# Down products of two signs as seven block products, in a Fourier mixing and gated expert kernel

## The chip, the cores and the metric

One core of a Trainium2 chip runs the whole program. The metric is the device time of one execution in microseconds. Before the change three runs took 1185.56, 1186.44 and 1188.01 us, the median is 1186.44. The core has TensorE (PE, with its weight loads shown as PEld), VectorE (DVE), ScalarE (ACT), GpSimd (POOL) and SyncE (SP, which here only issues transfers). TensorE writes to PSUM, a memory of eight banks of 512 fp32 columns in 128 partitions; ACT and DVE read and write both PSUM and SBUF; GpSimd works in SBUF.

## The reference

The input `x` is 8 x 3136 x 256. It is mixed by a Fourier transform over the sequence and one over the features, of which the real part is kept. The 25088 rows that result go through a feed-forward block with a softmax gate and a layer norm:

```python
X = np.fft.fft(np.fft.fft(x, axis=1), axis=2).real       # (8, 3136, 256)
h = X.reshape(25088, 256) @ w_in                          # 1024 wide
e = np.exp(h - h.max(-1)); sm = e / (e.sum(-1) + 1e-9)
solu = h * sm
ln = (solu - solu.mean(-1)) / np.sqrt(solu.var(-1) + 1e-6) * g_ln
out = ln @ w_out                                          # (25088, 256)
```

## The kernel before

**Transforms.** The eight sequences are worked on as four pairs. A sequence position is n = 64 n1 + n2 with 49 values of n1 and 64 of n2. The first transform (`transform1`, L171) goes over n1 for all n2, in sixteen pieces per pair; ACT copies each (L174) and SP writes it to a scratch in DRAM, from which `turn` (L187) loads it back with n2 on the partitions, five values of k1 at a time, into tiles of the pool `gpool`. The second transform (`transform2`, L199) goes over n2 for one k1 and gives 128 tokens; ACT copies the result to `q` (L205) and a small transfer, `spread`, puts one row of it to where VectorE wants it. The transform over features is folded into `w_in` at the start, with the even and odd halves of the features kept apart.

**Units and signs.** A unit is a pair and a k1 from 0 to 24: 100 units. The sum and the difference of the even and odd halves belong to k1 and to its mirror 49 - k1. These are the two signs of a unit; each sign has 128 tokens. Units with k1 = 0 have one sign.

**A unit's way.** `up` (L227) gives the even half in two PSUM banks, then the odd half in two others; `even` (L233, DVE) adds a rank-one term and puts the even half into SBUF; `join` (L241, DVE) makes h for each sign with its row maximum; `expo` (ACT) negates the maximum (L249) and takes the exponential (L251) with its sum; `product` (L259, DVE) multiplies h into it, giving u and the sum of u; GpSimd turns that sum to minus the mean (`nmean`, L264); `square` (L271, ACT) sums the squared deviations; `stats` (five small instructions on GpSimd) makes the scale rs of each token. Then u has to be transposed: DVE transposes blocks of 32 x 32 into `v` (`turn_blocks`, L299) and 16 transfers per batch of two units move the blocks to their places in `uT` (`move_blocks`, L325, SP). `uT` holds the two signs interleaved, element by element. `down` (L331) multiplies u of one sign, 128 x 1024, by `Wo`, 1024 x 256, in eight calls that sum in a PSUM tile; ACT scales the result by rs (`scale`, L336), and `store` writes it out, sign 0 from SP, sign 1 by an indirect transfer from GpSimd (L343). The layer norm's mean is taken out of `Wo` at the start (`centre`).

**Order.** The order of the instructions on every engine is the one in which the source issues them. Each engine works off its own list strictly in that order, and semaphores are set between engines where one uses what another made or still holds. The main loop has one step per unit, and a step works on units of different ages: step i issues `store` of unit i-5, then `up` and `even` of unit i, the second transform of unit i+2, then the joins and exponentials of unit i, the first transform of the next pair (`ahead_pe`), the down products of unit i-4 (`lag = 4`), the products, squares and block transposes of unit i, the scalings of unit i-4, the moves if the batch is full, `stats` of unit i, and for the next pair its loads, mirrored additions (`add_mirror`, L131, GpSimd) and folds (`fold`, DVE) in `ahead`. The first four units (`whole = 4`) are transposed on TensorE instead (`turn_whole`, L311), as there is no time yet for the moves. PSUM is full: four banks for `up`, four for everything else (`ps_m`).

Of the kernel before, what the change touches and what calls it, by code (L numbers as in the profile page):

```python
# [35 lines left out]
def kernel(  # L36
# [34 lines left out]
    gpool = ctx.enter_context(tc.tile_pool(name="gpool", bufs=6))  # L71
# [5 lines left out]
    ps_m = ctx.enter_context(tc.tile_pool(name="ps_m", bufs=4, space=PSUM))  # L77
# [5 lines left out]
    Wo = const.tile([P, KF, D], FP32, name="Wo")  # L83
    ones = const.tile([P, P], FP32, name="ones")
# [7 lines left out]

    class Pair:
        def __init__(self, p):
            self.p = p
            self.raw, self.y, self.y0 = {}, {}, None
            self.g, self.zs = {}, {}
# [45 lines left out]
    def transform1(pr, s):  # L145
# [6 lines left out]
        if l == 0:  # L152
# [3 lines left out]
            elif c < 4:  # L156
                z = fpool.tile([P, FF], FP32, tag="u", name="z_u", bufs=2)
                pr.z = z[0:ZR].rearrange("p (l d) -> p l d", l=CH)
            else:
                pr.z = gpool.tile([P, KG, D], FP32, tag="g", name="z_g")[0:ZR, 0:CH, :]  # L160
            pr.zs[c] = pr.z
        y = pr.y[c]
        ps = ps_m.tile([P, 2, D], FP32, tag="m", name="ps1")
        if s == NH // 2 - 1:
            parts = [(ps[0:ZR, 0], y[:, l], 0), (ps[0:ZR, 1], pr.y0[:, 0], 1), (ps[0:ZR, 1], y[:, l + 1], 2)]
        else:
            parts = [(ps[0:ZR], y[:, l : l + 2], 0)]
        first = True
# [67 lines left out]
    def join(t, ps):  # L236

        t.nmax = small.tile([P, 2], FP32, tag="nmax", name="nmax")
        for s in t.signs:
            t.h[s] = fpool.tile([P, FF], FP32, tag="h", name="h", bufs=2)  # L240
            nc.vector.tensor_tensor_reduce(out=t.h[s], in0=t.ev, in1=ps, scale=1.0, scalar=-3.0e38,  # L241
                                           op0=ALU.subtract if s else ALU.add, op1=ALU.max,
                                           accum_out=t.nmax[:, s : s + 1])
# [10 lines left out]
    def product(t, s, alone):  # L254

        if s == 0:
            t.usum = small.tile([P, 2], FP32, tag="usum", name="usum")
            t.nmean = small.tile([P, 2], FP32, tag="nmean", name="nmean")
        nc.vector.scalar_tensor_tensor(out=t.u[s], in0=t.h[s], scalar=1.0, in1=t.u[s], op0=ALU.mult,  # L259
                                       op1=ALU.mult, accum_out=t.usum[:, s : s + 1])  # L260
        if alone:
            nc.scalar.mul(out=t.nmean[:, s : s + 1], in_=t.usum[:, s : s + 1], mul=-1.0 / FF)
        else:
            nc.gpsimd.tensor_scalar(out=t.nmean[:, s : s + 1], in0=t.usum[:, s : s + 1], scalar1=-1.0 / FF,  # L264
                                    scalar2=None, op0=ALU.mult)

    def square(t, s):
# [3 lines left out]
        nc.scalar.activation(out=t.h[s], in_=t.u[s], func=ACT.Square, bias=t.nmean[:, s : s + 1],  # L271
                             accum_out=t.ssq[:, s : s + 1])

    def stats(t):
# [8 lines left out]
        nc.gpsimd.tensor_scalar(out=v[:, n], in0=t.ssq[:, n], scalar1=1.0 / FF, scalar2=None, op0=ALU.mult)  # L283
# [17 lines left out]
    def turn_whole(t):  # L301
# [4 lines left out]
        for s in t.signs:  # L306
            for half in range(2):
                ps = ps_m.tile([P, n, P], FP32, tag="m", name="ps_t")
# [17 lines left out]

    def down(t, s):
        uT = t.batch.uT[:, t.w].rearrange("p c i (n s) -> p c (i n) s", s=2)
        ps = ps_m.tile([P, D], FP32, tag="m", name="ps_o")
# [28 lines left out]
    mantissa = const.tile([P, NW], I32, name="mantissa")  # L358
# [13 lines left out]
    def exponent(w, raw):  # L372
# [3 lines left out]
        unit = qpool.tile([P, NW], I32, tag="unit", name="unit", bufs=3)  # L376
# [139 lines left out]
    def ahead_pe(pr, step):  # L516
# [5 lines left out]
        if 0 <= step - 20 < NK // KG:  # L522
            turn(pr, step - 20)

    with tc.manual_schedule():
# [82 lines left out]
        def begin(i):  # L608

            cur = units[i]  # L610
            if i % 2 == 0:
                batches.append(Batch(i >= whole))
            cur.batch, cur.w = batches[-1], i % 2
            even(cur, up(cur, 0))
            cur.odd = up(cur, 1)
            if i + 2 < len(units):
                nxt = units[i + 2]
                take2(nxt, transform2(pairs[nxt.p], nxt.k1))
                spread(nxt)
# [3 lines left out]
        for i in range(len(units) + lag):  # L623
            cur = units[i] if i < len(units) else None
            old = units[i - lag] if i >= lag else None
            ahd = pairs[cur.p + 1] if cur and cur.p + 1 < NP else None
# [131 lines left out]
```

## Time and profile before

| | |
|---|---|
| median of three runs | 1186.44 us |
| the profiled execution | 1185.83 us |
| its span, first to last instruction | 1183.7 us |
| TensorE clock granted | 1.00 |
| busy: PE, DVE, ACT, POOL | 1151.6, 904.6, 679.3, 494.1 us |
| down products on PE (L331) | 693.4 us, 3136 instructions |
| up products on PE (L227) | 360.5 us, 800 instructions |

A line of the groups reads: line, engine, operation, output <- inputs, shapes, count | busy us, mean ns of one | idle time of the engine ahead of them and what ended it. One fp32 matmul call of the source is two matmul instructions, each with a weight load. The mean of one matmul includes its way through the array, which overlaps the next matmul, so the rate is read from the length of a run and not from the mean. A line of a timeline reads: start, length, engine, line, operation, output <- inputs, shapes, count [idle before it <- what ended the idle time].

### The profile page before, as it was taken

The numbers are of one execution on the slowest core, as the hardware profiler recorded it, in microseconds if no ns is written. First come the engines' busy times: TensorE is split into PE (matmuls) and PEld (weight loads), VectorE is DVE, ScalarE is ACT, GpSimd is POOL, SyncE is SP. The second block draws the span as 40 slices with busy tenths as digits, with TensorE's granted clock in tenths as the row PEclk, the third lists the DMA queues.
The fourth block names the chain that finished last, engine by engine and source line by source line (L and its number), as shares of the span: only waits on it lengthen the run. The fifth ranks groups of instructions, "written<-read, shape, count | busy, mean of one in ns | idle before, by whom it ended". The sixth has DMA issues, their size and how long they took to land.

```text
span 1183.7 us, 15921 instructions
## 1 busy us (share of the span) xinstructions
PE 1151.6 (97%) x4720; PEld 873.9 (74%) x4720; DVE 904.6 (76%) x1234; ACT 679.3 (57%) x1411; POOL 494.1 (42%) x955
## 2 busy tenths in 40 slices
PE   2999999999999999999999999999999999999998
PEld 1557777777777777778777777777777777777787
DVE  7899777777868877877768878777777887777770
ACT  4577565555646665656546656565564665655561
POOL 3035545424435435333544444442543334333433
PEclk9999999999999999999999999999999999999999
DMA  9673868746875765654774775764684453534534
GB/s 241 200 180 75 209 157 194 199 126 155 193 184 139 192 177 140 177 149 130 179 189 133 194 177 144 171 173 113 163 196 123 119 144 103 148 107 124 142 90 118
DMA packets 458454, 185.39 MB, mean 157 GB/s; under 512 B 425750, under 2 KB 440350, under 8 KB 458368
## 3 DMA queue, kind: packets, MB, share of 16 engines
q1 hardware_dynamic: 444608, 146.22, 48.8%
q0 software_dynamic: 13760, 38.16, 11.8%
q8 instruction: 38, 0.62, 0.2%
q14 instruction: 48, 0.39, 0.1%
HBM read 44.78 MB, written 38.80 MB: 71 GB/s over the span
## 4 chain that ended last, share of the span: by engine, by line
PE 93%; DMA 3%; DVE 2%; ACT 1%; issue 1%; SPq 0%; DVEq 0%; ACTq 0%
PE ps_o L331 57%; PE ps_h L227 28%; PE ps L171 4%; PE ps L199 3%; DMA room<-in_x_dram 2%; DMA F<-in_f_tab_dram 1%; PE wps L462 1%; DVE u L259 0%; DVE h L241 0%; ACT h L271 0%; DVE y L123 0%; DVE ev L233 0%; ACT u L251 0%; DVE room L131 0%; DVE Wo L494 0%
## 5 line engine op out<-in xcount | busy, mean ns | idle before, releaser
L331 PE MATMUL ps_o<-Wo,uT 128*128 128x256 f32 x3136 | 693.4, 379 | 1.3 <-ACT uT L316 1.0
L331 PEld LDWEIGHTS ps_o<-Wo,uT 128*128 128x128 f32 x3136 | 611.2, 196 | 63.7 <-ACT uT L316 1.2
L227 PE MATMUL ps_h<-Wi,q 128*128 128x512 f32 x800 | 360.5, 593 | 2.3 <-DVE nmax L241 1.1
L259 DVE SCALAR_TENSOR_TENSOR u<-h,u 128x1024 f32<-128x1024 f32 x196 | 239.9, 1225 | 54.7 <-ACT u L251 27.7
L241 DVE CUSTOM_DVE_ANT_0 h<-ev,ps_h 128x1024 f32<-128x1024 f32 x196 | 231.7, 1219 | 49.8 <-PE ps_h L227 44.8
L227 PEld LDWEIGHTS ps_h<-Wi,q 128*128 128x128 f32 x800 | 151.6, 190 | 151.3 <-issue 142.0
L271 ACT ACTIVATE h<-u,nmean 128x1024 f32<-128x1024 f32 x196 | 225.0, 1149 | 57.8 <-POOL nmean L264 56.6
L264 POOL TENSOR_SCALAR nmean<-usum 128x1 f32<-128x1 f32 x189 | 78.5, 415 | 424.1 <-DVE u L259 423.5
L251 ACT ACTIVATE u<-h,neg 128x1024 f32<-128x1024 f32 x196 | 225.3, 1150 | 6.4
L299 DVE STREAM_TRANSPOSE v<-u 128x1024 f32<-128x1024 f32 x192 | 228.7, 1232 | 0.1
L233 DVE SCALAR_TENSOR_TENSOR ev<-w_mid,r,ps_h 128x1024 f32<-128x1024 f32 x100 | 127.8, 1278 | 132.1 <-PE ps_h L227 122.7
L205 ACT COPY q<-ps 128x256 f32<-128x256 f32 x100 | 37.1, 372 | 280.4 <-PE ps L199 253.2
L336 ACT ACTIVATE ot<-ps_o,rs 128x256 f32<-128x256 f32 x196 | 86.9, 461 | 60.4 <-PE ps_o L331 54.4
L343 POOL DMA_INDIRECT out_dram<-ot,idx x96 | 103.1, 1074 | 37.8 <-issue 22.4
L199 PEld LDWEIGHTS ps<-T,g 128*128 128x128 f32 x400 | 60.2, 191 | 47.4 <-issue 46.4
L171 PE MATMUL ps<-y,F 98*100 98x258 f32 (+3 forms) x288 | 71.3, 384 | 23.7 <-DVE y L124 23.7
L286 POOL TENSOR_TENSOR rs<-v,neg_half 128x2 f32<-128x2 f32 (+1 forms) x100 | 82.9, 829 | 7.8
L249 ACT ACTIVATE neg<-nmax 128x1 f32<-128x1 f32 x196 | 38.2, 195 | 63.7 <-DVE nmax L241 62.1
L283 POOL TENSOR_SCALAR v<-ssq 128x2 f32<-128x2 f32 (+1 forms) x100 | 23.7, 237 | 119.3 <-ACT h L271 119.3
L171 PEld LDWEIGHTS ps<-y,F 98*100 98x100 f32 x288 | 45.5, 177 | 35.8 <-DVE y L124 22.6
L199 PE MATMUL ps<-T,g 128*128 128x128 f32 x400 | 60.6, 275 | 0.0
L187 POOL DMA_DIRECT2D g<-zd x76 | 45.3, 608 | 28.8 <-DMA zd<-z_g 25.5
(73 smaller groups left out, 463.3 us busy)
## 6 DMA issues: line engine op xcount, KB each, us to landing
uT<-v SPq DMA_DIRECT2D x752, 128.0 KB
out_dram<-ot SPq DMA_DIRECT2D x100, 128.0 KB
g<-zd POOLq DMA_DIRECT2D x72, 160.0 KB, 4.0
xa<-in_x_dram SPq DMA_DIRECT2D x28, 392.0 KB
zd<-z SPq DMA_DIRECT2D x24, 400.0 KB
raw_in<-in_moe_w_in_dram SPq DMA_DIRECT2D x4, 512.0 KB
raw_out<-in_moe_w_out_dram SPq DMA_DIRECT2D x2, 1024.0 KB
r<-q SPq DMA_DIRECT2D x100, 0.5 KB
```

The source lines that it names most:

```text
L171: nc.tensor.matmul(o[..., cs], F[:, 2 * t + h, :], i[..., cs], start=first, stop=True, skip_group_check=True)
L199: nc.tensor.matmul(o, g[:, k, h * P : (h + 1) * P], table, start=(h == 0), stop=True, skip_group_check=True)
L227: nc.tensor.matmul(ps[:, fs], t.q[:, c * P : (c + 1) * P], Wi[:, c, fs], start=True, stop=True)
L233: nc.vector.scalar_tensor_tensor(out=t.ev, in0=w_mid, scalar=t.r, in1=ps, op0=ALU.mult, op1=ALU.add)
L241: nc.vector.tensor_tensor_reduce(out=t.h[s], in0=t.ev, in1=ps, scale=1.0, scalar=-3.0e38, op0=ALU.subtract if s else ALU.add, op1=ALU.max, ...
L251: nc.scalar.activation(out=t.u[s], in_=t.h[s], func=ACT.Exp, bias=t.neg[:, s : s + 1], accum_out=t.esum[:, s : s + 1])
L259: nc.vector.scalar_tensor_tensor(out=t.u[s], in0=t.h[s], scalar=1.0, in1=t.u[s], op0=ALU.mult, op1=ALU.mult, accum_out=t.usum[:, s : s + 1])
L271: nc.scalar.activation(out=t.h[s], in_=t.u[s], func=ACT.Square, bias=t.nmean[:, s : s + 1], accum_out=t.ssq[:, s : s + 1])
L299: nc.vector.transpose(out=t.batch.v[:, t.w, :, o], in_=t.u[s])
L331: nc.tensor.matmul(ps, uT[:, c, :, s], Wo[:, c, :], start=(c == 0), stop=(c == KF - 1))
L336: nc.scalar.mul(out=t.ot[s], in_=ps, mul=t.rs[:, s : s + 1])
L343: dma = nc.gpsimd.indirect_dma_start(out=out, out_offset=bass.IndirectOffsetOnAxis(ap=idx[:, i : i + 1], axis=0), in_=t.ot[s], in_offset=None)
```

## The change

The two signs of a unit are seen as one product: A, 256 tokens x 1024, by `Wo`, 1024 x 256. A is cut in four blocks of 128 x 512 (rows: sign; columns: half of the 1024), `Wo` in four of 512 x 128. Winograd's form of Strassen's scheme makes the four blocks of the result from seven block products, with four sums of blocks of A (`sums`, GpSimd, per unit, one step ahead of use) and four of blocks of `Wo` (`weight_sums`, once). The sums of products are made in PSUM: TensorE adds onto what is there, ACT copies a partial sum to a second place (C21), DVE adds a saved product (E5) to make C12 and C22. All units with two signs take this way but the last; the others keep `down`.

The products of a unit come in five pieces (`first` to `fifth`) between other work of the step. C11 and P5 lie in one PSUM bank, C21, C12 and C22 in another; `ps_m` shrinks to two banks for that. Squares and `stats` of a unit move to the next step; the mean's negation goes into the square's scale, so `nmean` disappears. The second transform and `spread` move to just before `fifth`; the loads of `turn` are spread over other steps, with three buffers for six. If the step has a piece of the first transform, both joins stand ahead of `both`, otherwise the second stands behind it.

```diff
-    gpool = ctx.enter_context(tc.tile_pool(name="gpool", bufs=6))
+    gpool = ctx.enter_context(tc.tile_pool(name="gpool", bufs=3))
...
-    ps_m = ctx.enter_context(tc.tile_pool(name="ps_m", bufs=4, space=PSUM))
+    spool = ctx.enter_context(tc.tile_pool(name="spool", bufs=2))
+    ps_m = ctx.enter_context(tc.tile_pool(name="ps_m", bufs=2, space=PSUM))
+    ps_s = ctx.enter_context(tc.tile_pool(name="ps_s", bufs=1, space=PSUM))
...
-        if alone:
-            nc.scalar.mul(out=t.nmean[:, s : s + 1], in_=t.usum[:, s : s + 1], mul=-1.0 / FF)
-        else:
-            nc.gpsimd.tensor_scalar(out=t.nmean[:, s : s + 1], in0=t.usum[:, s : s + 1], scalar1=-1.0 / FF,
-                                    scalar2=None, op0=ALU.mult)
...
-        nc.scalar.activation(out=t.h[s], in_=t.u[s], func=ACT.Square, bias=t.nmean[:, s : s + 1],
+        nc.scalar.activation(out=t.h[s], in_=t.u[s], func=ACT.Square, bias=t.usum[:, s : s + 1], scale=-float(FF),
                              accum_out=t.ssq[:, s : s + 1])
...
+    def weight_sums():
+
+        B11, B12, B21, B22 = [Wo[:, k : k + KF // 2, f : f + P] for k in (0, KF // 2) for f in (0, P)]
+        for j, (a, b) in enumerate(((B12, B11), (B22, Ws[:, 0]), (B22, B12), (B21, Ws[:, 1]))):
+            nc.gpsimd.tensor_tensor(out=Ws[:, j], in0=a, in1=b, op=ALU.subtract)
+
+    def blocks(t):
+        uT = t.batch.uT[:, t.w].rearrange("p c i (n s) -> p s c (i n)", s=2)
+        return [uT[:, s, c : c + KF // 2] for s in range(2) for c in (0, KF // 2)]
+
+    def sums(t):
+
+        A11, A12, A21, A22 = blocks(t)
+        t.S = spool.tile([P, 3, KF // 2, P], FP32, tag="S", name="S")
+        for o, a, b, op in ((t.S[:, 0], A21, A22, ALU.add), (t.S[:, 1], t.S[:, 0], A11, ALU.subtract),
+                            (t.S[:, 2], A12, t.S[:, 1], ALU.subtract), (A21, A11, A21, ALU.subtract)):
+            nc.gpsimd.tensor_tensor(out=o, in0=a, in1=b, op=op)
+
+    def block(o, a, b, start=False):
+        n = KF // 2
+        for c in range(n):
+            nc.tensor.matmul(o, a[:, c], b[:, c], start=start and c == 0, stop=c == n - 1, skip_group_check=True)
+
+    class Down:
+
+        def __init__(self, t, fresh):
+            self.t = t
+            a, b = (ps_s.tile([P, 2 * D], FP32, tag=f"s{i}", name=f"ps_s{i}") for i in range(2))
+            self.C11, self.P5 = a[:, 0:P], a[:, P : 2 * P]
+            self.C21, self.C12, self.C22 = (b[:, i * P : (i + 1) * P] for i in range(3))
+            self.A11, self.A12, self.S3, self.A22 = blocks(t)
...
+        def first(self):
+            t = self.t
+            block(self.C11, self.A11, Wo[:, 0 : KF // 2, 0:P], True)
+            block(self.P5, t.S[:, 0], Ws[:, 0])
+            nc.scalar.copy(self.C21, self.C11)
+            self.E5 = small.tile([P, P], FP32, tag="E5", name="E5", bufs=2)
+            nc.scalar.copy(self.E5, self.P5)
+
+        def second(self):
+            block(self.C11, self.A12, Wo[:, KF // 2 :, 0:P])
+            block(self.C21, self.t.S[:, 1], Ws[:, 1])
+            nc.vector.tensor_tensor(out=self.C12, in0=self.C21, in1=self.E5, op=ALU.add)
+            self.scale(0, 0, self.C11)
+
+        def third(self):
+            block(self.C21, self.S3, Ws[:, 2])
+
+        def both(self):
+            nc.vector.tensor_tensor(out=self.C22, in0=self.C21, in1=self.E5, op=ALU.add)
+
+        def fourth(self):
+            block(self.C12, self.t.S[:, 2], Wo[:, KF // 2 :, P:])
+            self.scale(0, 1, self.C12)
+
+        def fifth(self):
+            self.scale(1, 1, self.C22)
+            block(self.C21, self.A22, Ws[:, 3])
+            self.scale(1, 0, self.C21)
...
+    def turn_parts(pr, step):
+
+        if step in (-5, -3, 2, 6, 11):
+            turn(pr, (-5, -3, 2, 6, 11).index(step))
...
+        for i in range(whole + 1, len(units) + lag):
...
+            if i - lag + 1 < len(units) - 1 and len(units[i - lag + 1].signs) == 2:
+                sums(units[i - lag + 1])
+            if seven:
+                down7 = Down(old, i == whole + 1)
+                down7.first()
...
+            if prv:
+                for s in prv.signs:
+                    square(prv, s)
+                stats(prv)
+            store(units[i - lag - 1])
             if cur:
+                enter(i)
+                even(cur, up(cur, 0))
+            if seven:
+                down7.second()
...
+            if cur:
+                cur.odd = up(cur, 1)
+                more = len(pairs[min(cur.p + 1, NP - 1)].done)
+                other_pairs(i, ahead_pe)
+                more = len(pairs[min(cur.p + 1, NP - 1)].done) > more
+                join(cur, 0)
+                if more and 1 in cur.signs:
+                    join(cur, 1)
+            if seven:
+                down7.third()
+                down7.both()
+            if cur:
+                if not more and 1 in cur.signs:
+                    join(cur, 1)
+                expo(cur)
+            if seven:
+                down7.fourth()
+            if cur:
+                second_transform(i + 2)
+            if seven:
+                down7.fifth()
             if cur:
                 for s in cur.signs:
+                    product(cur, s)
+                for s in cur.signs:
+                    turn_blocks(cur, s)
...
+                for pr in pairs[1:]:
+                    turn_parts(pr, i - pr.p * NK)
+                other_pairs(i, ahead)
```

## The prediction, made before the changed kernel had run

> **What bounds the kernel now.** I read the page's busy shares and the chain that ended last, then the groups of instructions on TensorE, then a timeline of two steps engine by engine.
>
> ```profile
> PE 1151.6 (97%) x4720; PEld 873.9 (74%) x4720; DVE 904.6 (76%) x1234; ACT 679.3 (57%) x1411; POOL 494.1 (42%) x955
> ...
> PE 93%; DMA 3%; DVE 2%; ACT 1%; issue 1%; SPq 0%; DVEq 0%; ACTq 0%
> ...
> L331 PE MATMUL ps_o<-Wo,uT 128*128 128x256 f32 x3136 | 693.4, 379 | 1.3 <-ACT uT L316 1.0
> ...
> L227 PE MATMUL ps_h<-Wi,q 128*128 128x512 f32 x800 | 360.5, 593 | 2.3 <-DVE nmax L241 1.1
> ```
>
> TensorE is busy 97% of the span, carries 93% of the chain, and its two big groups wait 1.3 and 2.3 us in all. The down product alone is 693 of 1152 us. The other engines have slack.
>
> ```profile
> 54.56 1.05 PE L199 MATMUL ps<-T,g 128*128 128x128 f32 x8
> ...
> 73.23 1.91 PE L311 MATMUL ps_t<-ident,u 128*128 128x128 f32 x16
> ...
> 605.71 3.60 PE L227 MATMUL ps_h<-Wi,q 128*128 128x512 f32 x8
> 609.15 0.61 PE L199 MATMUL ps<-T,g 128*128 128x128 f32 x4
> 609.59 7.08 PE L331 MATMUL ps_o<-Wo,uT 128*128 128x256 f32 x32
> 616.51 3.60 PE L227 MATMUL ps_h<-Wi,q 128*128 128x512 f32 x8
> ```
>
> An fp32 matmul call is two instructions. A run's length less its last instruction (379, 593, 275 ns), over the others, is the interval: (7.08 - 0.38)/31 = 0.216 us for 256 columns, (3.60 - 0.59)/7 = 0.43 for 512, (1.05 - 0.28)/7 = 0.11 for 128 with a new weight load each. So one step (one unit) is 3.43 (up) + 0.44 (second transform) + 6.91 (down) = 10.8 us, which is 616.51 - 605.71; a step that also holds a first transform (L171) is 0.86 longer.
>
> ```profile
> 598.65 1.22 DVE L241 CUSTOM_DVE_ANT_0 h<-ev,ps_h 128x1024 f32<-128x1024 f32 x1 [0.53 <-PE ps_h L227]
> ...
> 601.48 1.23 DVE L259 SCALAR_TENSOR_TENSOR u<-h,u 128x1024 f32<-128x1024 f32 x1 [0.46 <-issue]
> ```
>
> ```profile
> 599.91 0.20 ACT L249 ACTIVATE neg<-nmax 128x1 f32<-128x1 f32 x1 [0.54 <-DVE nmax L241]
> 600.15 1.15 ACT L251 ACTIVATE u<-h,neg 128x1024 f32<-128x1024 f32 x1
> ...
> 601.52 1.15 ACT L251 ACTIVATE u<-h,neg 128x1024 f32<-128x1024 f32 x1
> 602.57 0.19 ACT L251 ACTIVATION_READ_ACCUMULATOR u<-h,neg 128x1 f32 x1
> 606.42 0.81 ACT L336 ACTIVATE ot<-ps_o,rs 128x256 f32<-128x256 f32 x2
> ```
>
> Here one sees the chain join, exponential, exponential: ACT is through with both about 4.0 us after the first join starts (602.67 against 598.65). Today nothing on TensorE waits for it; the down product in flight belongs to a unit four steps older.
>
> **The change part by part: TensorE's work.** Removed per unit: 32 instructions of 256 columns, 32 x 0.216 = 6.91 us. Added: seven blocks of 4 calls, 56 instructions of 128 columns, at 0.112 each = 6.27 us. Ends for that 0.112: 0.109 (run of 16 transposes) and 0.121 (scaled by the 197 ns that a load of uT takes against 190 for others). 0.112 is from the nearest row, fp32 with a load per matmul. If nothing waits: -0.64 us for each of 95 units, -61 us.
>
> **The change's waits.** The blocks are not one run: they are five pieces with ACT and DVE work on the same PSUM tile in between. C21, C12 and C22 share one tile, 384 of the 512 columns of one bank. What decides is whether accesses of different engines to *other columns* of that bank are kept in source order. I take it that they are, since a PSUM tile's bank is one unit for the waits that the program gets. The trace of before can't show it: there each PSUM tile is written whole by TensorE and then read. So I bound it from both sides: no such wait (the first rival), or all of them (my case).
>
> The Trainium skill ("PSUM — Partial Sum Buffer", PSUM bank collisions raise a hardware error) says that two engines must not be in one bank and quadrant at once, also at disjoint columns, and tells to guard by bank. No run here shows a collision; by this rule the waits below must be there and the step is the longer one, by column-wise waits it would be the shorter one.
>
> With bank order the last piece (`fifth`, block C21) waits for ACT's scaling of C22, and in ACT's order that stands behind both exponentials of the current unit, the scaling of C12 and the copy of q. One step, in us from the start J of the first join, which is 0.30 after TensorE has issued `up`'s odd half (598.65 against 598.35):
> - TensorE: `third` from -0.30 to 0.60. `fourth` must wait for `both` on DVE (bank order), which follows the first join: 1.15 to 1.5 (a 98x127 add takes 0.28; with a PSUM operand I take 0.35). `fourth` 1.55 to 2.45, second transform to 2.9. Idle so far 0.95.
> - ACT: negated maximum 1.26, exponential 1.49, and again 2.72 and 2.95 (the second join now stands behind `both`); free at 4.1. Scaling of C12 +0.25, q +0.3, scaling of C22 done at 5.0. A 128x256 scaling has 0.36 between issues and a 128x1 activation about 0.1, so 0.25 lies between; this is the estimate of the walk with most room, 0.1 to 0.36 each.
> - TensorE: `fifth` from 5.05 to 6.05 (the first matmul after a wait costs 0.1 more). Idle 2.15 more. Behind it stand the next step's `first` (16 x 0.112 = 1.79), `up` even 1.72, `second` 1.79, `up` odd 1.72: the next join starts at 6.05 + 7.02 + 0.30 = 13.35.
>
> So the step is a loop of about 13.3 us in place of 10.8: join, two exponentials, scalings, `fifth`, `first`, up, `second`, up, join. 10.1 us of it is TensorE work and 3.1 is waiting. A first transform (0.86) falls into the wait, so steps with one are 13.3 too, where they were 11.65.
>
> **The rest, inside this loop.** *Squares a step later* and `stats` behind them: on ACT from about 8.5 to 10.9 of the walk, done before the next join at 13.3 needs the buffers of h; rs is wanted three steps on. They cost nothing while the step is over 11; nmean's 189 POOL instructions (78.5 us busy, mostly waiting) go, and ACT's 7, off the path. *The two copies* (C21, E5) after `first`: by 8.5, needed by `second` at 9.6. *Two DVE adds* at 0.35: DVE's step is 8.6 + 0.7, under 13.3; without that cover its own loop (join to join over products, transposes, even) is 9.8. *Block sums on POOL*: rows of 1020 and 765 elements take 2341 and 1795 ns, so 512 take 1.25 us, four 5.0 a step. With stats 2.0, a store 1.3, and mirrored adds (2.5) and gathers (1.2) in every second step, POOL has some 10.6 us a step, under 13.3. The sums' waits: uT one step earlier than now. The 16 moves of a batch take SP 11.1 us to issue from the last transpose (J + 7.8), so about J + 21 with landing; the sums are wanted as of J + 33. Queued behind a waiting sum are stats, store and mirrored adds, all with a step or more of room.
>
> The skill ("GPSIMD Engine Reference", Key points) warns of contention with VectorE instructions that have two SBUF inputs. The adds of 1020 elements on POOL lie within 2333 to 2370 ns whether VectorE's joins and evens overlap them or not, but those read one side from PSUM; the products (two SBUF inputs) never overlapped them, so that case isn't shown.
>
> *`turn` in other steps, three buffers for six*: the same 4 loads of 0.6 us each on POOL, each several steps ahead of use: nothing, and without that room 2.4 us five times a pair. *spread* later in the step: SP's queue has the store and 16 moves before and after it, 12.5 us in 26; r is used two steps later. *Start* (weight sums once, 5 us of POOL, buffers shared): 0 to +2, covered by TensorE's start gaps; I take +1.
>
> **The sum, against the profiled execution** (1185.83 us, span 1183.7; median of the runs 0.6 above). Steps 5 to 99 run now from 95.06 to 1151.8, 1056.7 us. After: 89 steps x 13.3 = 1183.7; three whose current unit has one sign, one exponential (1.37) less, 36; three whose old unit has one sign and no blocks, bound by DVE's 9.8 loop, about 30. Sum 1249.7, +193. Tail: units 96 to 98 have nobody's work between the pieces; 6.27 + waits of about 0.85, 0.6, 0.6, 0.9 = 9.2 for 6.91, +7. Start +1. 1185.8 + 201, from the median 1387 us.
>
> **Rivals.**
> - *Waits go by columns, not by bank* (ends on the other side). Then `fifth` waits only for `both`, which ends at 1.5 while TensorE is at 2.2; a step is 10.15 or 11.0, TensorE stays full: 1186 - 61 + 5 (tail) + a few for DVE in steps with folds = about 1135. For it: DVE's loop of 9.8 just fits under 10.15. It decides at a wait of 0.64 us per step: any more and the change loses. Against it: one bank per tile.
> - *POOL becomes the bound*. uT is read at every second float and one sum is written there; no row has that. If a sum takes twice 1.25, POOL needs 15.6 us in the 48 steps that also load ahead: 48 x 2.3 = +110, about 1495. It binds above 1.9 us per sum.
> - *The 128-column blocks go at the load's own 196 ns*: 40 of the 56 instructions are in the loop, +3.4 us a step, about 1700. Against it: the run of 16 above at 0.109.
>
> **How the numbers follow.** Bank order 0.83, columns 0.10, POOL 0.05, loads 0.02. For the likeliest case the step may be off by 0.4 (scalings 0.1 to 0.36, waits some 0.05 each) x 92 = 37 us, and up to +33 if 0.121 is the interval: 1345 to 1445. I give 1340 to 1455, with a little for POOL above; that leaves out columns, most of POOL, loads and a tail of my case, together 2 in 10. A measurement of this kernel tells about 0.2% from no change. Faster 0.10, same 0.01, slower 0.89.
>
> **What would show it.** Right: TensorE busy near 80% with its idle before `fifth`'s matmuls, put down to ACT's `ot`; steps of 13.3 with and without a first transform; 56 block instructions a step at 0.11 within a piece; POOL busy rising to some 0.75 of the span with waits on matmuls or copies, none that TensorE waits for. Wrong: TensorE still at 97%, and `fourth` starting before `both` has ended, would mean that columns count; TensorE waiting for the sums, that POOL does.

## The result, and the profile after

The changed kernel takes 1429.38 us (median of four runs, 1424.56 to 1437.76) against 1186.6 us before (1185.56 to 1188.01): 1.2053 times as long, interval 1.1994 to 1.2112. The profiled execution took 1430.68 us with a span of 1428.7 us; the mean granted clock of TensorE was 0.978, where it had been 1.000.

The page of the changed kernel, busy shares, granted clock (PEclk, in tenths for each of 40 slices of the span) and groups (columns as before):

```profile
PE 1187.9 (83%) x7002; PEld 928.3 (65%) x7002; DVE 1042.8 (73%) x1424; ACT 740.9 (52%) x1784; POOL 1051.3 (74%) x1150
...
PEclk9999999999999999999999999999999899999989
...
L272 DVE SCALAR_TENSOR_TENSOR u<-h,u 128x1024 f32<-128x1024 f32 x196 | 324.7, 1674 | 29.5 <-ACT u L265 24.8
L362 PE MATMUL ps_s<-Ws,uT 128*128 128x128 f32 x1520 | 227.2, 294 | 125.7 <-ACT ot L410 120.5
...
L362 PE MATMUL ps_s<-Ws,S 128*128 128x128 f32 x1520 | 206.2, 280 | 1.6 <-POOL S L357 1.6
L362 PE MATMUL ps_s<-Wo,S 128*128 128x128 f32 x760 | 111.0, 289 | 75.5 <-DVE ps_s L398 75.5
```

TensorE has gone from 97% busy to 83%. Two block groups hold most of its idle time: 120.5 us wait for ACT's scaling into `ot` (L410), ahead of `fifth`; 75.5 us wait for DVE's addition in `both` (L398), ahead of `fourth`. By the list of waits each of the two comes 95 times, once in every unit that goes by blocks; the longest took 2.0 and 1.3 us. One step on TensorE, from one `up` (L241) to the next:

```profile
700.44 1.88 PE L241 MATMUL ps_h<-Wi,q 128*128 128x512 f32 x4
702.16 1.10 PE L362 MATMUL ps_s<-Wo,uT 128*128 128x128 f32 x8
703.09 1.06 PE L362 MATMUL ps_s<-Ws,S 128*128 128x128 f32 x8
703.98 1.88 PE L241 MATMUL ps_h<-Wi,q 128*128 128x512 f32 x4
705.70 1.10 PE L362 MATMUL ps_s<-Ws,uT 128*128 128x128 f32 x8
707.50 1.16 PE L362 MATMUL ps_s<-Wo,S 128*128 128x128 f32 x8 [0.69 <-DVE ps_s L398]
708.49 0.61 PE L213 MATMUL ps<-T,g 128*128 128x128 f32 x4
710.95 1.21 PE L362 MATMUL ps_s<-Ws,uT 128*128 128x128 f32 x8 [1.85 <-ACT ot L410]
711.99 1.11 PE L362 MATMUL ps_s<-Wo,uT 128*128 128x128 f32 x8
712.93 1.06 PE L362 MATMUL ps_s<-Ws,S 128*128 128x128 f32 x8
713.83 1.88 PE L241 MATMUL ps_h<-Wi,q 128*128 128x512 f32 x4
```

In order: `up` even, `second` (702.16 and 703.09), `up` odd, `third` (705.70), `fourth` (707.50), the second transform, `fifth` (710.95), and the next step's `first` (711.99 and 712.93). The step is 713.83 - 700.44 = 13.39 us where it was 10.79. Why `fifth` starts at 710.95 is seen on ACT in the same stretch:

```profile
707.26 0.20 ACT L263 ACTIVATE neg<-nmax 128x1 f32<-128x1 f32 x1 [3.56 <-DVE nmax L255]
707.50 1.15 ACT L265 ACTIVATE u<-h,neg 128x1024 f32<-128x1024 f32 x1
...
708.87 1.15 ACT L265 ACTIVATE u<-h,neg 128x1024 f32<-128x1024 f32 x1
...
710.01 0.35 ACT L410 ACTIVATE ot<-ps_s,rs 128x128 f32<-128x128 f32 x1
710.26 0.36 ACT L219 COPY q<-ps 128x256 f32<-128x256 f32 x1
710.51 0.38 ACT L410 ACTIVATE ot<-ps_s,rs 128x128 f32<-128x128 f32 x1
```

The scaling of C22 (the second L410) ends at 710.89, and `fifth` starts 0.06 us later. It writes other columns, C21, of the same bank. The scaling had to wait for nothing of its own: C22 was complete at 707.44, when `both` ended on DVE:

```profile
707.14 0.30 DVE L398 TENSOR_TENSOR ps_s<-ps_s,E 128x128 f32<-128x128 f32 x1
```

It stands in ACT's list behind both exponentials, the scaling of C12 and the copy of q.

Where the time went, span against span: 245.0 us more. 4.9 lie ahead of step 5, 228.6 in steps 5 to 98 (from 1046.4 to 1275.0 us), 11.5 in the last step and the tail. Of those 94 steps, 65 take 13.2 to 13.5 us.

### The profile page after: what moved, and what is told of

Read it like the earlier page. It is cut to its first block, busy times and chain, and to the rows that moved or that the text cites. A ratio compares the mean times of both kernels' runs of the same rounds, so it can differ in the third digit from the quotient of the medians.

```text
span 1428.7 us, 21631 instructions
## 1 busy us (share of the span) xinstructions
PE 1187.9 (83%) x7002; PEld 928.3 (65%) x7002; DVE 1042.8 (73%) x1424; ACT 740.9 (52%) x1784; POOL 1051.3 (74%) x1150
## 5 line engine op out<-in xcount | busy, mean ns | idle before, releaser
L241 PE MATMUL ps_h<-Wi,q 128*128 128x512 f32 x800 | 379.9, 599 | 3.1 <-DVE ev L247 2.2
L272 DVE SCALAR_TENSOR_TENSOR u<-h,u 128x1024 f32<-128x1024 f32 x196 | 324.7, 1674 | 29.5 <-ACT u L265 24.8
L362 PE MATMUL ps_s<-Ws,uT 128*128 128x128 f32 x1520 | 227.2, 294 | 125.7 <-ACT ot L410 120.5
L362 PEld LDWEIGHTS ps_s<-Ws,uT 128*128 128x128 f32 x1520 | 206.9, 202 | 170.8 <-ACT ot L410 138.7
L357 POOL TENSOR_TENSOR S<-uT 128x512 f32<-128x512 f32 x95 | 147.8, 1555 | 207.6 <-DMA out_dram<-ot 84.2
L362 PEld LDWEIGHTS ps_s<-Wo,uT 128*128 128x128 f32 x1520 | 209.5, 204 | 50.3 <-issue 44.4
L279 ACT ACTIVATE h<-u,usum 128x1024 f32<-128x1024 f32 x196 | 224.4, 1154 | 6.3 <-DVE u L272 6.2
L362 PE MATMUL ps_s<-Wo,uT 128*128 128x128 f32 x1520 | 218.5, 289 | 4.4 <-ACT E L386 1.7
L410 ACT ACTIVATE ot<-ps_s,rs 128x128 f32<-128x128 f32 x380 | 138.0, 364 | 149.1 <-PE ps_s L362 142.3
L241 PEld LDWEIGHTS ps_h<-Wi,q 128*128 128x128 f32 x800 | 139.4, 193 | 105.7 <-issue 100.4
L362 PE MATMUL ps_s<-Ws,S 128*128 128x128 f32 x1520 | 206.2, 280 | 1.6 <-POOL S L357 1.6
L362 PEld LDWEIGHTS ps_s<-Ws,S 128*128 128x128 f32 x1520 | 190.6, 197 | 2.0 <-POOL S L357 2.0
L362 PE MATMUL ps_s<-Wo,S 128*128 128x128 f32 x760 | 111.0, 289 | 75.5 <-DVE ps_s L398 75.5
L357 POOL TENSOR_TENSOR S<-uT,S 128x512 f32<-128x512 f32 x95 | 149.7, 1576 | 7.5
L357 POOL TENSOR_TENSOR uT<-uT 128x512 f32<-128x512 f32 x95 | 138.5, 1458 | 0.0
```

The source lines that it names most:

```text
L241: nc.tensor.matmul(ps[:, fs], t.q[:, c * P : (c + 1) * P], Wi[:, c, fs], start=True, stop=True)
L357: nc.gpsimd.tensor_tensor(out=o, in0=a, in1=b, op=op)
L362: nc.tensor.matmul(o, a[:, c], b[:, c], start=start and c == 0, stop=c == n - 1, skip_group_check=True)
L410: nc.scalar.mul(out=self.t.ot[s][:, half * P : (half + 1) * P], in_=ps, mul=self.t.rs[:, s : s + 1])
```

## The experiments

### The scalings out of the way

Theory: bank order puts `fifth` behind ACT's scalings. Moving these behind the last block in the source takes away what `fifth` waits for and leaves the work as it is.

```diff
         def fourth(self):
             block(self.C12, self.t.S[:, 2], Wo[:, KF // 2 :, P:])
-            self.scale(0, 1, self.C12)
         def fifth(self):
-            self.scale(1, 1, self.C22)
             block(self.C21, self.A22, Ws[:, 3])
+            self.scale(0, 1, self.C12)
+            self.scale(1, 1, self.C22)
             self.scale(1, 0, self.C21)
```

> The changed kernel with one thing moved: ACT's scalings of C12 and C22 stand behind the last block (C21) in the source, not ahead of it. Bank order (my theory): the wait of the last piece on ACT (120 us of TensorE idle, put down to ot) goes. What is left is the wait of fourth for both, 0.7 us without a first transform and 1.2 with one: steps of about 11.2 and 12.2, 1215 to 1260 us. Rival, the sums on POOL and the longer products on DVE set the step: it stays above 1400 us. Rival, column order: ACT's order was no cause, 1430 us.

Measured: 1319.19 us (1316.57 to 1326.86), 1.1139 times before (1.1099 to 1.1178): 110 us of the loss gone. TensorE's timeline:

```profile
712.21 1.16 PE L362 MATMUL ps_s<-Wo,S 128*128 128x128 f32 x8 [0.70 <-DVE ps_s L398]
713.21 0.61 PE L213 MATMUL ps<-T,g 128*128 128x128 f32 x4
713.65 1.11 PE L362 MATMUL ps_s<-Ws,uT 128*128 128x128 f32 x8
```

`fifth` (713.65) now follows the second transform at once, and TensorE's waits for `ot` have fallen from 120.5 to 2.4 us in all. The shortest steps are 11.28 us without a first transform and 12.42 with one. But the time is 59 us above the upper end of what the theory had given: many steps are 0.6 to 4 us longer than these floors. Something else waits as soon as the loop is shorter; runs further down look for it.

The other test of the same theory moves one block of the result to another bank, and nothing else:

```diff
-            self.C21, self.C12, self.C22 = (b[:, i * P : (i + 1) * P] for i in range(3))
+            self.C21, self.C12 = (b[:, i * P : (i + 1) * P] for i in range(2))
+            self.C22 = a[:, 2 * P : 3 * P]
```

> The changed kernel with C22 in the bank of C11 and P5 instead of that of C21 and C12; nothing else moves. Bank order: the last piece now waits for the scaling of C12, which ACT does 0.5 us earlier (ahead of the copy of q and the scaling of C22), so steps of 12.9 instead of 13.4, 1375 to 1395 us. Column order: no wait depends on the place, 1425 to 1435 us.

Measured: 1370.75 us (1369.64 to 1373.06), ratio 1.1553 (1.1533 to 1.1572), 59 us less than the change and 4 under the range that bank order gave. On its TensorE, `fifth` and the next `up`:

```profile
709.18 1.21 PE L362 MATMUL ps_s<-Ws,uT 128*128 128x128 f32 x8 [1.31 <-ACT ot L411]
...
712.06 1.88 PE L241 MATMUL ps_h<-Wi,q 128*128 128x512 f32 x4
```

The wait of `fifth` fell from 1.85 to 1.31 us and the usual step from 13.39 to 12.86: `fifth` now waits only for the scaling of C12, which is still in its bank. Had waits gone by columns, the move would have changed nothing. So it is shown twice that other columns of the same bank are waited for. A PSUM tile of these two is a whole bank, so no run tells the bank from the tile as the unit; and a program with waits by columns was not tried.

### The cost of one block

The products of the kernel before, in two halves of 128 columns each: the same arithmetic, in the size of the blocks and with the same strided `uT`, with no wait added.

```diff
-        for c in range(KF):
-            nc.tensor.matmul(ps, uT[:, c, :, s], Wo[:, c, :], start=(c == 0), stop=(c == KF - 1))
+        for f in range(0, D, P):
+            for c in range(KF):
+                nc.tensor.matmul(ps[:, f : f + P], uT[:, c, :, s], Wo[:, c, f : f + P], start=(c == 0 and f == 0),
+                                 stop=(c == KF - 1), skip_group_check=True)
```

> The kernel before with each down product made in two halves of 128 columns, 64 instructions a unit where there were 32: it prices the 128-column matmul with its own weight load, strided weights included. At 0.112 us a step grows by 0.26: 1205 to 1215 us. At 0.121: +0.8 a step, 1265 us. At the load's 0.196: +5.6 a step, 1730 us.

Measured: 1246.68 us (1245.66 to 1247.24), ratio 1.0505 (1.0487 to 1.0523), between the two expectations. The group of its page, which waits for nothing worth naming:

```profile
L332 PE MATMUL ps_o<-Wo,uT 128*128 128x128 f32 x6272 | 754.2, 281 | 1.0 <-ACT uT L316 1.0
```

Its steps are 11.42 and 12.28 us, 0.63 more than before, so 64 instructions take 6.91 + 0.63 = 7.54 us, 0.118 each. In the changed kernel the runs say the same: eight instructions of a block from `uT` take 1.10 us, (1.10 - 0.275)/7 = 0.118; eight from the sums, which lie without gaps, 1.06 us, 0.112. A unit has 32 of the one and 24 of the other: 6.46 us, so seven block products save 0.45 us of TensorE's 6.91, not an eighth (0.86).

### What the sums on GpSimd cost

Three runs leave the sums out, in the change, in `scales_last`, and in `pieces_joined` (below): a constant tile stands for them.

```diff
-        t.S = spool.tile([P, 3, KF // 2, P], FP32, tag="S", name="S")
-        for o, a, b, op in ((t.S[:, 0], A21, A22, ALU.add), (t.S[:, 1], t.S[:, 0], A11, ALU.subtract),
-                            (t.S[:, 2], A12, t.S[:, 1], ALU.subtract), (A21, A11, A21, ALU.subtract)):
-            nc.gpsimd.tensor_tensor(out=o, in0=a, in1=b, op=op)
+        if not kept:
+            kept.append(spool.tile([P, 3, KF // 2, P], FP32, tag="S", name="S"))
+            nc.gpsimd.memset(kept[0], 0.5)
+        t.S = kept[0]
```

> The changed kernel without the block sums of u on POOL (the products read a constant tile instead, so the output is not the reference's). Bank order: POOL and the longer products are off the path, steps stay 13.4; the product on DVE goes back from 1.67 to 1.22 us; 1405 to 1430 us, the difference from steps behind units of one sign. Contention theory (POOL and DVE share something, and that is the time): under 1350 us.

Measured: 1420.78 us (1417.23 to 1425.2), ratio 1.1963 (1.1943 to 1.1983). That is 8.6 us under the change, with ranges that touch (1417.23 to 1425.2 and 1424.56 to 1437.76). The product on DVE went from 1674 to 1291 ns on average, but the regular steps stay at 13.39 and 13.42 us: under this loop the sums are nearly hidden.

> scales_last without the block sums on POOL (a constant tile is read in their place, the output is not the reference's). scales_last has steps of 11.28 and 12.42 us as its floor, with many that are 0.6 to 4 longer. Theory, the sums: they and DVE's products slow each other (1.8 and 1.9 us each), and TensorE then waits for a sum or for DVE; without them nearly all steps are at the floor, 1255 to 1275 us. Rival, the longer steps come from transfers (r, uT) or stores that are late by themselves: 1300 to 1320 us.

Measured: 1265.53 us (1264.29 to 1266.95), ratio 1.0654 (1.0636 to 1.0672). Nearly all steps are now at their floors, 11.28 and 12.42 us. So 54 of the 1319 us of `scales_last` come from the sums: hidden under a 13.4 us loop, not under one of 11.3 to 12.4.

Part of the way they do it is on DVE. The product (L272) with two sums of GpSimd beside it, in the changed kernel:

```profile
708.77 1.85 DVE L272 SCALAR_TENSOR_TENSOR u<-h,u 128x1024 f32<-128x1024 f32 x1 [0.21 <-ACT u L265]
...
710.56 2.30 DVE L272 SCALAR_TENSOR_TENSOR u<-h,u 128x1024 f32<-128x1024 f32 x1
```

GpSimd in the same stretch, and two sums of the next step that no product overlaps:

```profile
708.26 1.29 POOL L357 TENSOR_TENSOR S<-S,uT 128x512 f32<-128x512 f32 x1
709.63 2.15 POOL L357 TENSOR_TENSOR S<-uT,S 128x512 f32<-128x512 f32 x1
711.74 2.02 POOL L357 TENSOR_TENSOR uT<-uT 128x512 f32<-128x512 f32 x1
...
719.98 1.29 POOL L357 TENSOR_TENSOR S<-uT,S 128x512 f32<-128x512 f32 x1
721.23 1.04 POOL L357 TENSOR_TENSOR uT<-uT 128x512 f32<-128x512 f32 x1
```

and a product of `no_sums`:

```profile
706.45 1.23 DVE L272 SCALAR_TENSOR_TENSOR u<-h,u 128x1024 f32<-128x1024 f32 x1
```

Each slows the other: the product goes from 1.23 to 1.85 and 2.30, the third sum from 1.29 to 2.15, the fourth from 1.04 to 2.02. The ends show how. The product that starts at 708.77 ends at 710.62, 1.07 us after the sum that was running when it started (709.55); the next sum ends 1.16 later, the next product 1.08 after that, the last sum 0.90 after that. So the two engines take turns, one whole instruction at a time: in the traces of this kernel, `scales_last`, `pieces_joined`, `sums_alone` and `sums_act_mean`, of the 533 products that started while a sum had at least 0.2 us to go, 532 ended 1.08 to 1.09 us after that sum. In `scales_last` the two meet more often, and TensorE waits for the sums too. Its groups:

```profile
L272 DVE SCALAR_TENSOR_TENSOR u<-h,u 128x1024 f32<-128x1024 f32 x196 | 371.9, 1917 | 29.1 <-ACT u L265 24.2
...
L362 PE MATMUL ps_s<-Ws,S 128*128 128x128 f32 x1520 | 208.8, 282 | 19.1 <-POOL S L357 19.1
```

### Fewer waits still

`pieces_joined` is `scales_last` with `third` and `fourth` in one piece, `both` behind them, and the first transform behind the exponentials. `fourth` then waits no longer for `both`; `more` tells as before whether the step has a piece of the first transform.

```diff
-                more = len(pairs[min(cur.p + 1, NP - 1)].done)
-                other_pairs(i, ahead_pe)
-                more = len(pairs[min(cur.p + 1, NP - 1)].done) > more
+                more = cur.p + 1 < NP and any(cur.k1 - 2 - c in (0, 1) for c in START[cur.p + 1 == 1])
                 join(cur, 0)
...
             if seven:
                 down7.third()
+                down7.fourth()
                 down7.both()
             if cur:
                 if not more and 1 in cur.signs:
                     join(cur, 1)
                 expo(cur)
-            if seven:
-                down7.fourth()
-            if cur:
+                other_pairs(i, ahead_pe)
                 second_transform(i + 2)
```

> scales_last with third and fourth issued back to back, both behind them, and the first transform's piece after the exponentials (ahead of fifth). Bank order: TensorE's wait for both falls from 0.7 and 1.2 us to about 0.2, so TensorE's own step is 10.6 or 11.2. If the sums on POOL slow DVE as they do in scales_last, DVE's loop of 10.1 grows by 1.5 or so and sets the step: 1200 to 1260 us. If they don't matter: 1150 to 1165 us, faster than before.

Measured: 1317.5 us (1316.27 to 1321.91), ratio 1.1106 (1.1083 to 1.1128), no better than `scales_last`. The floors did fall, to 10.53 and 11.18 us, under the 10.79 and 11.65 of before, but only about a quarter of the steps reach them: products take 1897 ns on average, and TensorE's waits for the sums have grown from 19.1 to 37.9 us. Its wait for `both` is down from 75.5 us in the change to 2.0. It also waits 23.6 us for the addition of C12 on DVE and 12.5 for rs, which `stats` makes behind the sums in GpSimd's queue; without the sums (`joined_no_sums`, below) these are 3.4 us and nothing. The order of the pieces on TensorE was no longer the main thing that set the time.

A small GpSimd instruction that reads the last product's row sum, ahead of the sums, was to keep the sums clear of the products:

```diff
+                if prv:
+                    gate = small.tile([P, 2], FP32, tag="gate", name="gate", bufs=2)
+                    n = slice(0, len(prv.signs))
+                    nc.gpsimd.tensor_scalar(out=gate[:, n], in0=prv.usum[:, n], scalar1=1.0, scalar2=None, op0=ALU.mult)
                 sums(units[i - lag + 1])
```

> pieces_joined with one tiny instruction on POOL ahead of the block sums, which waits for the sum that DVE's last product of the unit before gives: the sums then start behind the products. Theory, what costs is sums and products at the same time: the products are back at 1.2 to 1.5 us and the kernel takes 1165 to 1210 us, at least 30 under pieces_joined. Rival, POOL's amount of work is what counts, not when it comes: the same as pieces_joined or slower, as POOL waits more.

Measured: 1325.17 us (1322.66 to 1326.83), ratio 1.1159 (1.114 to 1.1179). The rival had given this number, but the run decides little: the products still took 1908 ns, so the gate did not part the two, and sums clear of products were not tested.

> pieces_joined without the block sums on POOL (a constant tile is read in their place, the output is not the reference's). pieces_joined has floors of 10.53 and 11.18 us a step but many steps 1 to 5 longer. Theory, sums and products slowing each other is all that is left: nearly all steps at the floor, 1175 to 1195 us, so that even without this cost the scheme would about equal the kernel before. Rival, the long steps come from the order of the pieces itself: 1290 to 1320 us.

Measured, with the sums left out: 1228.52 us (1220.95 to 1231.36), ratio 1.0333 (1.0289 to 1.0376). Neither expectation: most steps are at the floors of 10.53 and 11.18, but some stretches are not. In one of them TensorE stops ahead of `first`:

```profile
603.03 2.04 PE L363 MATMUL ps_s<-Wo,uT 128*128 128x128 f32 x8 [4.64 <-issue]
604.86 1.92 PE L363 MATMUL ps_s<-Ws,S 128*128 128x128 f32 x8
```

The profile names no releaser for these 4.64 us; `uT` of the next batch was being moved, with the DMA engines busy 92% of the time from 597.18 to 603.03, which speaks for the moves but does not show them; the granted clock from there to 609.53 was 0.54. Even with its two big waits and its sums taken out, the scheme in this arrangement is 3% slower than the kernel before. Against `pieces_joined` 89 us went with the sums.

### The sums without the scheme

The sums put into the kernel before, where nobody reads them (they go into a tile S of their own, for which `gpool` has five buffers instead of six, and the fourth sum is not written over `uT`):

```diff
+            if lag < i < len(units) + lag - 2 and len(units[i - lag + 1].signs) == 2:
+                sums(units[i - lag + 1])
```

> The kernel before, with the four block sums of each unit made on POOL as well, into tiles that nobody reads (the fourth not over uT). Theory: they lengthen DVE's products (1.22 us now, 1.5 to 2 then), DVE and POOL have the slack, TensorE waits for neither: 1186 to 1200 us. Rival, the sums cost time by themselves, through DVE or through POOL's other work: over 1220 us.

Measured: 1421.75 us (1419.39 to 1423.16), ratio 1.1971 (1.1947 to 1.1995). A large miss of my expectation. GpSimd's list in this kernel:

```profile
700.73 1.51 POOL L334 TENSOR_TENSOR S<-uT 128x512 f32<-128x512 f32 x1
702.32 2.15 POOL L334 TENSOR_TENSOR S<-S,uT 128x512 f32<-128x512 f32 x1
704.55 2.16 POOL L334 TENSOR_TENSOR S<-uT,S 128x512 f32<-128x512 f32 x1
706.67 1.04 POOL L334 TENSOR_TENSOR S<-uT 128x512 f32<-128x512 f32 x1
707.88 1.14 POOL L352 DMA_INDIRECT out_dram<-ot,idx  x1 [0.18 <-issue]
709.03 2.37 POOL L188 DMA_DIRECT2D g<-zd  x4
711.42 0.46 POOL L265 TENSOR_SCALAR nmean<-usum 128x1 f32<-128x1 f32 x2
```

and the first line of its waits:

```profile
ACT h L272 <- POOL nmean L265: 638.4, 92, 10.1
```

`nmean`, two instructions of 0.23 us, stands behind 7 us of sums, a store and four loads; the square on ACT waits for it, and what stands behind the square on ACT holds TensorE up: 71.3 us for scalings, whose PSUM tiles it needs, and 80.9 us for ACT's copies (L125) that the first transform reads. With `nmean` computed on ACT that queue is out of the way:

```diff
-                    product(cur, s, i < whole)
+                    product(cur, s, True)
```

> sums_alone (the kernel before with the block sums on POOL, unread) with nmean made by ACT instead of POOL, so that no step of a unit's chain stands behind the sums in POOL's queue. Theory, the queue: sums_alone's 235 us come from squares on ACT that wait for nmean behind the sums; with it gone the kernel is near the one before, 1190 to 1215 us, though sums and products still lengthen each other (1.7 to 2 us). Rival, the cost is the sharing of something between POOL and DVE: 1350 to 1420 us.

Measured: 1207.97 us (1206.08 to 1210.08), ratio 1.0188 (1.0169 to 1.0207); most steps are back at 10.79 and 11.65 us. So of the 235 us that unread sums cost, 1421.75 - 1207.97 = 214 were the queue, with the lower clock that came with it (0.947 granted in the profiled execution, 0.995 without the queue), and 22 are the rest, the slower products among it (1560 ns on average).

### The lowered clock

Some steps of the changed kernel take 14.9 us, with waits no longer than elsewhere: 20, 47 and 51, and then every sixth, 85, 91 and 97. TensorE in step 85:

```profile
1188.79 0.61 PE L213 MATMUL ps<-T,g 128*128 128x128 f32 x4
1191.24 1.95 PE L362 MATMUL ps_s<-Ws,uT 128*128 128x128 f32 x8 [1.84 <-ACT ot L410]
1192.99 1.91 PE L362 MATMUL ps_s<-Wo,uT 128*128 128x128 f32 x8
1194.69 1.13 PE L362 MATMUL ps_s<-Ws,S 128*128 128x128 f32 x8
```

and two stretches of the same kernel (length, busy time of PE, PEld, DVE, ACT and POOL, granted clock, DMA share, GB/s):

```profile
1191.24:1194.69 3.45, 3.45 (x16) 3.45 (x17) 3.45 (x6) 0.37 (x1) 3.03 (x6) 0.53 0.02 0
1196.10:1209.50 13.40, 10.86 (x70) 8.58 (x69) 8.90 (x13) 6.96 (x19) 10.45 (x15) 1.00 0.72 172
```

For these 3.45 us the granted clock is 0.53 on average, and eight instructions take 1.95 instead of 1.21 us; then it is 1.00 again. (The lowered stretch proper is 3.41 us at 0.50, from 1191.43.) The theory: the idle time of each step brings this about. Twelve matmuls that nobody reads fill it in the steps without a first transform, where alone steps of 14.9 us were seen:

```diff
+            if cur and seven and not more:
+                ps = ps_m.tile([P, 2 * D], FP32, tag="m", name="ps_f")
+                for c in range(6):
+                    nc.tensor.matmul(ps[:, 0:P], ident, Wo[:, c, 0:P], start=True, stop=True, skip_group_check=True)
             if seven:
                 down7.fifth()
```

> The changed kernel with 12 matmuls of 128 columns that nobody reads (1.35 us) put into TensorE's wait of 1.85 us before the last piece, in the steps that have no first transform. The steps of 14.9 us that the changed kernel has now and then show a granted clock below 1. Theory, TensorE's idle time lowers its clock: the long steps go and the clock is 1.00, 1405 to 1415 us. Rival, the long steps have another cause: 1425 to 1435 us, clock 0.98.

Measured: 1421.83 us (1413.56 to 1424.59), ratio 1.199 (1.197 to 1.201), in between the two expectations, with granted clocks of 0.988 to 0.996 against 0.977 to 0.983. In its profiled execution the steps 85, 91 and 97 take 13.39 us:

```profile
1192.84 1.50 PE L816 MATMUL ps_f<-Wo,ident 128*128 128x128 f32 x12
1194.85 1.21 PE L362 MATMUL ps_s<-Ws,uT 128*128 128x128 f32 x8 [0.50 <-ACT ot L410]
```

and steps 5 to 98 sum to 1259.2 us, 15.8 less than in the change. The idle time has to do with the lowered clock; the median gives 8 us for it, and the ranges touch (1413.56 to 1424.59 and 1424.56 to 1437.76).

Why one step and not the next is seen in the clock records of the traces. All lowered stretches of a run begin on one grid of 3.41 us and last one, two or three cells of it: those of steps 85, 91 and 97 begin at 1191.43, 1273.35 and 1355.27, 24 cells apart. In the cell ahead of the first, from 1188.02, TensorE was busy 1.57 of 3.41 us, 46%, as it holds the whole wait before `fifth`. Over the thirteen traces, from 60 us on, of the cells at full clock with TensorE busy under 45%, 68 of 71 were followed by a lowered one; of those busy 52% or more, none of 4437; in between, 40 of 112. A step of 13.39 us is 3.92 cells, so the wait shifts against the grid from step to step and falls into one cell only now and then. Five such steps and the long one are 81.88 us, 24 cells are 81.92: hence every sixth.

## Why the prediction was right, and where it was not

The prediction was 1387 us (1340 to 1455, slower at 0.89); 1429 us was measured, inside the range, 42 us above. The loop that it named is the one that sets the step, and the walk through it came out to about 0.1 us at the points given below. That the total lies inside the range is in part luck: the room was set for the scalings, the waits and a dearer block, and most of the 42 us came from the lowered clock and from irregular steps, for which it had no term. The prediction's own terms, 37 us either way and 33 more upwards, give 1350 to 1457, not its 1345 to 1445.

- *The waits* (bank order, `fifth` behind the exponentials). Right, and shown by `scales_last` and `c22_other_bank` for `fifth`, and by `pieces_joined` for `fourth`, whose wait went from 75.5 to 2.0 us. The walk through one step, from the first join's start at 706.00: the scaling of C22 ended at +4.89 (5.0 predicted), `fourth` started at +1.50 (1.55), `fifth` at +4.95 (5.05), and the next join came at +13.39 (13.35). The two copies ended at +8.5 and the squares lay from +8.4 to +10.8, as in the walk. Steps with a first transform took 13.42, as predicted no longer than those without. The Trainium skill ("PSUM — Partial Sum Buffer", PSUM bank collisions raise a hardware error) tells to guard PSUM by bank and quadrant and not by address. The waits of this program fit that, also at other columns of a bank; no run here shows a collision. The price is from the trace: 75.5 us in all for one such wait per unit, 120.5 for the other.
- *TensorE's work*, -0.64 us a unit. The mis-sized term: 0.112 holds for the blocks of sums alone, those of `uT` take 0.118, so it is -0.45. The two given ends, 0.109 and 0.121, held it, but the upper one does not follow from its source: 0.112 scaled by 197/190 is 0.116, under the measured 0.118. In the walk this is 0.1 of the 8.1 us from `fifth` to the next `third`, and `fifth` starting 0.1 earlier made up for most of it.
- *The sum over the steps*, 1236 us for steps 5 to 98 (1249.7 less one step of 13.3). 1275.0 measured: 39 of the 44 us by which the profiled execution exceeds its sum (1186 + 201). The steps were taken at 13.3 and not at the walk's own 13.35 (its terms add up to 13.37); they are 13.40, which is 88 x 0.1 = 9 us. About 16 are the lowered clock, which the prediction did not have, by what `filler` took off (1275.0 - 1259.2). Some 17 are a dozen steps that are longer by 0.4 to 5 us, next to those with a one-signed unit (28, 30, 53, 55, 78, 80) and a few others (15, 18, 19, 44, 68, 69), which the walk took as regular. Of these, 15, 18, 19, 44 and 69 are 0.5 to 0.9 us longer than the usual 11.65 in the kernel before as well; the causes were not followed. The three steps whose old unit has one sign were 5 us cheaper than the 30 set for them. Start: 4.9 us against 1. Last step and tail: 11.5 against 10 (3 and 7).
- *DVE's additions* 0.30 us for 0.35; *scalings* 0.25 apart on ACT, as taken; *POOL* busy 74% for 75%, TensorE 83% for "near 80%"; idle 0.69 and 1.85 us by the profile against 0.95 and 2.15, where the walk counts from the end of issue and the profile from the modelled end of the last matmul; counted as in the walk they are 0.86 and 2.01.
- *The sums*, 1.25 us each. Without a product beside them they took 1.51, 1.30, 1.33 and 1.07 us on average, 5.2 a step for the 5.0 predicted; over all, 1.44 to 1.58, 6.0 a step. The contention that the prediction had called not shown is there, but under 13.4 us it is nearly free: TensorE waited 1.6 us in all for the sums of `first` and `second`. The skill's warning ("GPSIMD Engine Reference", Key points) on instructions with two SBUF inputs is borne out by the product's 1.23 against 1.85 and 2.30 us.
- *Squares a step later, `nmean` gone*, costed at nothing. In the step above they end at +10.8, clear of the next join at +13.39. But I had not seen what they are for: `sums_alone` and `sums_act_mean` show that in the kernel before, where `nmean` stands in GpSimd's queue, the sums alone cost 235 us, 214 of them by that queue.
- *The rivals.* Columns (1135 us): excluded. Its number would have been too low as well: `pieces_joined` has nearly its steps as floors, 10.53 and 11.18 against 10.15 and 11.0, and took 1317 us. POOL as the bound above 1.9 us per sum: sums reach that only beside a product, and TensorE's waits for them were 1.6 us; in a shorter loop, with 19.1 and 37.9 us, the rival begins to hold. The price of a strided operand, for which the rival had allowed twice 1.25, is 1.51 us with both inputs at every second float. Blocks at 196 ns: excluded by `halves`.

## What to carry to other kernels

A product with fewer operations that has to go in pieces, with other engines' work on the same accumulator in between, turns a run without waits into a loop through those engines' queues: price every piece by what stands ahead of it on the engine that releases it, here two exponentials of another unit, and take the PSUM bank (here also the tile) as the unit of waiting, not the columns. Work on an engine with slack is free only while the loop is long and nothing on the path stands behind it in that queue: the same sums cost about 9 us in the change as it is, 54 with its loop shortened and 235 ahead of a 0.2 us instruction that ACT needed. Before building it, measure the smaller operation alone: an eighth fewer operations was 0.45 us of 6.91.

## What the runs showed of the hardware

- TensorE's granted clock fell to 0.50 for 3.41 us at a time although the wait ahead of it in steps 85, 91 and 97 was 1.84 us. What the lowered stretches have ahead of them is a cell of a 3.41 us grid in which TensorE was busy about half the time or less (68 of 71 cells under 45%, none of 4437 from 52% up). The Trainium skill ("TensorE: Matmul & The Clock Gate", HAM oscillation — how this bites in real kernels) puts the danger at gaps of more than about 3.4 us; here the length of a lowered stretch fits that figure, the gaps that went before do not.
- fp32 matmuls of 128 columns with a weight load each go at 0.112 us from a tile without gaps and at 0.118 from one read at every second float.
- A DVE instruction of 128 x 1024 with two SBUF inputs takes 1.25 us on average in the changed kernel where no sum of GpSimd overlaps it (71 products) and 2.01 where sums overlap at least 95% of it (75 products): it waits for the sum that is running to end and then takes 1.08 us. Joins, with one PSUM input, stay at 1.22, and transposes at 1.22 to 1.24.
